# Two more token blocks of a gated layer in Strassen's seven-product form, with attention and weight decoding moved in the schedule

## Chip, cores and metric

One core of one Trainium2 chip runs the whole program in one launch. The metric is the device time of that launch in microseconds (us); lower is better. The time before is the median of three runs.

## What is computed

Pooled attention, then two gated layers, all in float32; the five weight matrices arrive as 64-bit floats. Cut to what matters:

```python
k_p = k.reshape(B, H, Sp, 8, D).mean(axis=3)         # B=8 batches, H=8 heads, S=576, D=64
v_p = v.reshape(B, H, Sp, 8, D).mean(axis=3)         # Sp = 72
attn = softmax(q @ k_p.T / sqrt(D))
x = (attn @ v_p) -> [B*S, H*D]                       # 4608 tokens x 512
x = ((x @ w_a) * (x @ w_b)) @ w_out                  # first layer, d_ff = 1536
h = x @ w_in                                         # second layer, d_ff = 2048
out = (h * clip(h + 3, 0, 6) / 6) @ w_out2
```

## The kernel before

**Tiling.** The 4608 tokens are NB = 9 blocks of 512 (TB). A matrix product in full precision is three matmuls of 128x128 by 512 (mm3, L724: high by high, low by high, high by low); block 0 alone uses single float32 matmuls. The two products x @ w_a and x @ w_b of the first layer are called the gates here.

**Plain blocks.** The first PLAIN = 5 blocks (L72) run step(j, f) (L932) for each of the NF1 = 12 slices f of 128 hidden columns: gate a into PSUM (pa), copied by ScalarE (asb, L959); gate b (pb), multiplied by VectorE (L982); the product split into a high and a low part (L84, L85); and y_part (L743), which adds the slice's share of the output in four PSUM banks that stay open over all 12 slices. The weights of gate b and of w_out come from DRAM in every block from block 2 on (w1_load, L719), those of gate a stay in SBUF.

**Superblocks.** The other blocks go in pairs of 1024 tokens, NSUP = (NB - PLAIN) // 2 of them. pair1(s, p) (L1498) runs six times in a superblock (NP1 = 6), each time on two slices f and for both gates m, over the seven products of Strassen's scheme (ORDER). x_prod (L1416) is one product of one gate: 2 x 3 matmuls. x_evict (L1433) takes results out of PSUM: ScalarE copies, VectorE adds and multiplies, GpSimd multiplies and subtracts. y_chunk (L1459) makes a 128-row share of the output for 512 tokens (2 x 3 matmuls), eight in a pair, which VectorE adds to an SBUF sum (ya, L1471) from the second pair on. The seven combinations of the weights (ab) are made once, in superblock 0, from the weights read back with t_load (L1300), by t_step (L1309), on ScalarE, VectorE and GpSimd, and stored to DRAM (tdram); later superblocks load them (L1320) LEAD = 3 products ahead. The combinations of the input are made by x_make (L1361) in seven pieces, from blocks that x_load (L1351) reads back from DRAM (xdram).

**The hand-made order.** Every engine and the DMA queue of SyncE (SP) work in the order in which this program issues. The clock of that order is the slot: a plain step has 3 slots, so a block has SLOTS = 36, and a pair of a superblock has 12, so a superblock has 72. With PLAIN = 5, superblock 0 starts at slot 180, superblock 1 at 252, and the second layer follows at 324. Attention is cut into 40 chunks of up to 128 tokens; `base` (L546 to L550) gives each chunk a first slot. The loop after it places the parts of a chunk: loads seven slots ahead, q_tr and scores (PE, VectorE), expo (ScalarE), sums, normal (GpSimd), at_main, at_left (PE, ScalarE, VectorE), and pv (PE, ScalarE), which for blocks from XD = 3 on stores the result to xdram. The first chunk of a batch also brings the pooling of k (k_prep, four VectorE reductions, nine to six slots ahead) and of v (v_prep, vl_prep). The 4 + 5 + 6 + 3 + 4 + 5 + 5 + 5 + 3 chunks of the blocks 0 to 8 start as follows: block 2 in slots 26 to 46, blocks 3 to 6 in slots 50 to 151, blocks 7 and 8 in slots 184 to 220. Batches 3, 4, 5 and 6 start within slots 50 to 151, batch 7 at 199. x_load and t_load of superblock 0 are at slots 166 and 169, its x_make pieces from 171 on.

**Weights of the second layer.** They are decoded from 64 bits and combined in 2 x NF2 = 32 steps: w2_stage (load), w2_decode and w2_end (ScalarE, VectorE, GpSimd), and for every two steps w2_sums (VectorE) and w2_make (ScalarE, VectorE, GpSimd, then stores to DRAM). W2_STEPS = 20 of them run in the plain blocks, one every two steps f from the fourth step of block 1 on; the other 12 in the last superblock, one every four slots (w2_slot, L1477).

run_slot(s, hold) (L629) issues what is planned for a slot; with hold it puts the pooling (k_prep, v_prep, vl_prep) off to run_held (L638).

Of the kernel before, what the change touches and what calls it, by code (L numbers as in the profile page):

```python
# [25 lines left out]
def pooled_attention_then_two_moe_kernel(  # L26
# [24 lines left out]
    NF2 = F2 // P  # L51
# [3 lines left out]
    NB = NT // TB  # L55
# [13 lines left out]
    ident = const.tile([P, P], F32, name="ident")  # L69
    masks = const.tile([P, 4], F32, name="masks")  # L70
    ydram = [dpool.tile([P, NCC, TB], F32, name=f"ydram{j}") for j in range(NB)]
    PLAIN = 5  # L72
    XD = 3
    NSUP = (NB - PLAIN) // 2
    xdram = {j: dpool.tile([P, NCC, TB], F32, name=f"xdram{j}") for j in range(XD, NB)}
# [430 lines left out]
    chunks, pieces, chunk_piece, block_chunks = [], [], {}, [[] for _ in range(NB)]  # L506
    for b in range(B):
        t = 0
        while t < S:
            j, r = divmod(b * S + t, TB)  # L510
            seg = S - t if b > 1 else min(S - t, TB - r)
            while seg:
                j = (b * S + t) // TB
# [16 lines left out]

    SLOTS = 3 * NF1
    SPAN2 = (26, 46)
    SPANS = ((50, 151), (184, 220))
    X_AT = 166
    T_AT = 169
    X0_AT = (171, 173, 174, 176, 177, 179, 180, 182)
    plan = {}

    def at(slot, fn, *args):
# [2 lines left out]
    def spread(cs, first, last):  # L542
        n = len(cs)
        return [first + i * (last - first) // max(1, n - 1) for i in range(n)]

    base = [None] * len(block_chunks[0])  # L546
    base += [4 * i + 6 for i in range(len(block_chunks[1]))]
    base += spread(block_chunks[2], *SPAN2)
    base += spread([c for j in range(3, PLAIN + 2) for c in block_chunks[j]], *SPANS[0])
    base += spread([c for j in range(PLAIN + 2, NB) for c in block_chunks[j]], *SPANS[1])  # L550
    att_used = {}
    WIDE = block_chunks[3][0]

# [10 lines left out]
    for c, (b, t0, n) in enumerate(chunks):  # L564
# [30 lines left out]
        x = place(max(s0, done) + 1, (scores, c, 0), (scores, c, 1))  # L595
# [4 lines left out]
        x = place(x + 5 + 2 * wide, (at_main, c), (at_left, c))  # L600
# [26 lines left out]
    held = []  # L627

    def run_slot(s, hold=False):  # L629
        now[0] = s  # L630
        calls = sorted(plan.pop(s, ()), key=lambda x: rank(x[0]))
        for fn, args in calls:
            if hold and fn in (k_prep, v_prep, vl_prep):
                held.append((fn, args))
            else:
                fn(*args)

    def run_held():  # L638
# [54 lines left out]

    AHEAD = 2
    W2_FROM = 3
    W2_STEPS = 20
    xd_t = {}

    def x_fetch(j):
# [774 lines left out]

    YWORK = (1, 1, 2, 1, 1, 1, 1)

    def w2_slot(x):  # L1477

        i, ph = divmod(x, 4)
        i += W2_STEPS  # L1480
        if x < 0 or i > 2 * NF2 + 1:
            return
        if ph == 0 and i < 2 * NF2:
            w2_stage(i)
        if W2_STEPS < i <= 2 * NF2:
            if ph == 1:
                w2_decode(i - 1)
            elif ph == 2:
                w2_end(i - 1)
        if i >= W2_STEPS + 2 and i % 2 == 0 and ph == 3:  # L1490
            w2_sums(i // 2 - 1, 0)
        if i >= W2_STEPS + 2 and i % 2 and ph in (0, 2):
            w2_make(i // 2 - 1, ph // 2)

    prev1 = []
    w2_late = []

    def pair1(s, p):  # L1498
# [3 lines left out]
        last = s == NSUP - 1  # L1502
# [4 lines left out]
        def hook(hold=False):  # L1507
            nonlocal section
            for u in range(section * 12 // 14, (section + 1) * 12 // 14):
                if u % 3 == 0:  # L1510
                    flush()
                if last and (p, u) == P2_AT:
                    attn_stack.close()
                    p2.append(ctx.enter_context(tc.tile_pool(name="p2", bufs=1)))
                if last and hold:
                    w2_late.append(4 * 3 * p + u - 6)
                elif last:
                    while w2_late:
                        w2_slot(w2_late.pop(0))
                    w2_slot(4 * 3 * p + u - 6)  # L1520
                run_slot(slot0 + u, hold)
            if not hold:
                while w2_late:
                    w2_slot(w2_late.pop(0))
                run_held()
            section += 1

# [94 lines left out]
```

## Time and profile before

| | us |
|---|---|
| median of 3 runs | 1738.91 |
| lowest and highest run | 1736.78, 1739.81 |
| span of the profiled execution, first to last instruction | 1736.1 |
| TensorE (PE) busy in it | 1701.8 |

Only the span of the profiled execution is on the page; its own time from outside is not given. The runs' median is 2.8 us above the span. Times within a profile count from the span's start. Stretches in it, read from the starts of the blocks' matmuls and evictions: block 1 from 181 to 307, block 2 to 427, block 3 to 541, block 4 to 643, superblock 0 to 832, superblock 1 to 1022, then the second layer. A view by windows gives the busy time of each engine in a stretch; a group of instructions gives their number and mean duration; PE's matmul durations overlap each other, so the rate of matmuls is read from how many lie in a stretch in which PE is never idle.

### The profile page before, as it was taken

What the parts mean: (1) busy time and instruction counts of PE and PEld (TensorE: products, weight loads), DVE (VectorE), ACT (ScalarE), POOL (GpSimd) and SP (SyncE); (2) the same over time, 40 slices, a digit from 0 to 9 for tenths busy, and PEclk for the clock granted to TensorE, in tenths of its full rate; (3) what the DMA queues carried; (4) which work ended last, traced back from release to release, by engine and by line L of the source; (5) the groups of instructions that cost most, each with busy time, mean ns of one, the idle gap of its engine ahead of it and who ended that gap; (6) DMA issues with size and microseconds to landing.
All of it is one profiled execution on the core that took longest, in us unless ns stands there. A gap on an engine that the chain in (4) does not pass through costs nothing.

```text
span 1736.1 us, 24577 instructions
## 1 busy us (share of the span) xinstructions
PE 1701.8 (98%) x7924; PEld 1371.8 (79%) x7924; DVE 1247.7 (72%) x1978; ACT 787.5 (45%) x1622; POOL 918.6 (53%) x779
## 2 busy tenths in 40 slices
PE   7989999999999999999999999999999999999998
PEld 5445788787887887888888877888888888888898
DVE  6777877667758467754666776687678768767776
ACT  6655444333334344443344434455445545544453
POOL 4565223113213147666545627686577668666753
PEclk9999999999999999999999999999999999999999
DMA  9774558796878667755688948465945976594896
GB/s 255 196 227 128 175 190 263 190 313 183 273 264 293 210 243 249 247 183 213 216 294 281 343 154 317 172 227 152 319 155 180 239 276 217 155 315 157 300 293 256
DMA packets 294480, 404.31 MB, mean 233 GB/s; under 512 B 157392, under 2 KB 197840, under 8 KB 294352
## 3 DMA queue, kind: packets, MB, share of 16 engines
q1 hardware_dynamic: 293920, 402.22, 71.2%
q8 instruction: 64, 1.05, 0.2%
q14 instruction: 64, 0.52, 0.1%
q10 hardware_dynamic: 432, 0.52, 0.1%
HBM read 307.23 MB, written 95.42 MB: 232 GB/s over the span
## 4 chain that ended last, share of the span: by engine, by line
PE 79%; DVE 7%; DMA 5%; issue 3%; SPq 2%; ACT 2%; POOL 2%; DVEq 0%; POOLq 0%; ACTq 0%
PE y L728 4%; PE y L726 4%; PE y L727 4%; PE oZ L728 4%; PE phZ L726 4%; PE oZ L726 4%; PE phZ L727 4%; PE phZ L728 4%; PE oZ L727 4%; PE phX L726 3%; PE phX L728 3%; PE phX L727 3%; PE oX L727 2%; PE oX L726 2%; PE oX L728 2%
## 5 line engine op out<-in xcount | busy, mean ns | idle before, releaser
L85 POOL TENSOR_TENSOR g<-r,g 128x512 fp32r<-128x512 f32 (+1 forms) x192 | 254.0, 1345 | 10.0 <-ACT g L84 10.0
L1161 POOL TENSOR_TENSOR r<-r,r 128x512 f32<-128x512 f32 (+1 forms) x39 | 47.2, 1211 | 181.1 <-DVE rT L1159 152.2
L98 POOL TENSOR_TENSOR w2f<-w2f,w2st 128x512 int32<-128x512 int32 x32 | 42.7, 1334 | 153.7 <-ACT w2st L91 101.9
L1192 DVE TENSOR_TENSOR oacc<-oZ,oacc 128x512 f32<-128x512 f32 (+1 forms) x130 | 82.5, 635 | 52.6 <-PE oZ L728 52.3
L726 PE MATMUL oZ<-g,wo 128*128 128x512 f32 (+1 forms) x320 | 118.4, 370 | 1.3 <-DVE oacc L1192 1.3
L728 PE MATMUL oZ<-g,wo 128*128 128x512 f32 (+1 forms) x320 | 118.5, 370 | 0.9 <-POOL g L85 0.5
L727 PE MATMUL oZ<-g,wo 128*128 128x512 f32 (+1 forms) x320 | 118.0, 369 | 0.0
L84 ACT CAST g<-r 128x512 fp32r<-128x512 f32 (+1 forms) x195 | 104.5, 576 | 16.4 <-DVE r L1163 15.9
L85 POOL TENSOR_TENSOR g<-rT,g 128x512 fp32r<-128x512 f32 (+1 forms) x77 | 98.1, 1275 | 20.5 <-ACT g L84 18.1
L1137 ACT ACTIVATE r<-phX 128x512 f32<-128x512 f32 (+1 forms) x78 | 43.2, 554 | 128.7 <-DVE phX L1131 126.5
L726 PE MATMUL phZ<-Sh,wi 128*128 128x512 f32 x256 | 99.9, 390 | 1.5 <-ACT r L1137 1.5
L1471 DVE TENSOR_TENSOR ya<-y,ya 128x512 f32<-128x512 f32 x80 | 54.9, 687 | 64.3 <-PE y L728 64.3
L728 PE MATMUL phZ<-Sl,wi 128*128 128x512 f32 x256 | 99.8, 390 | 0.0
L727 PE MATMUL phZ<-Sh,wi 128*128 128x512 f32 x256 | 99.7, 389 | 0.0
L959 ACT COPY asb<-pa 128x512 f32<-128x512 f32 x60 | 35.2, 586 | 114.6 <-PE pa L728 93.5
L726 PE MATMUL pa<-xh,wa 128*128 128x512 f32 x192 | 76.9, 400 | 0.0
L728 PE MATMUL y<-g,wo 128*128 128x512 f32 x192 | 75.0, 391 | 0.9 <-POOL g L85 0.8
L726 PE MATMUL phX<-Sh,wi 128*128 128x512 f32 x192 | 74.9, 390 | 0.5 <-ACT e L1127 0.5
L728 PE MATMUL pa<-xl,wa 128*128 128x512 f32 x192 | 75.1, 391 | 0.0
L727 PE MATMUL pa<-xh,wa 128*128 128x512 f32 x192 | 75.0, 391 | 0.0
L726 PE MATMUL y<-g,wo 128*128 128x512 f32 x192 | 74.9, 390 | 0.0
L728 PE MATMUL phX<-Sl,wi 128*128 128x512 f32 x192 | 74.9, 390 | 0.0
(947 smaller groups left out, 5491.5 us busy)
## 6 DMA issues: line engine op xcount, KB each, us to landing
wo<-wod SPq DMA_DIRECT2D x140, 512.0 KB
wi<-wsd SPq DMA_DIRECT2D x120, 512.0 KB
tdram<-ab SPq DMA_DIRECT2D x42, 512.0 KB
ab<-tdram SPq DMA_DIRECT2D x42, 512.0 KB
wod<-tt SPq DMA_DIRECT2D x56, 256.0 KB
wsd<-tt SPq DMA_DIRECT2D x24, 512.0 KB
wo<-w1dram SPq DMA_DIRECT2D x24, 512.0 KB
wi<-wsd SPq DMA_DIRECT2D x40, 256.0 KB
```

Source lines behind the costliest of these rows:

```text
L84: (hi_eng or nc.scalar.copy)(hi, src)
L85: (lo_eng or nc.gpsimd).tensor_tensor(lo, src, hi.bitcast(F32), ALU.subtract)
L98: nc.gpsimd.tensor_tensor(di, di, lo.bitcast(I32), ALU.add)
L726: nc.tensor.matmul(o, wh, xh, start=first, stop=False, skip_group_check=more)
L727: nc.tensor.matmul(o, wl, xh, start=False, stop=False, skip_group_check=more)
L728: nc.tensor.matmul(o, wh, xl, start=False, stop=last, skip_group_check=more)
L959: nc.scalar.copy(asb, pa)
L1137: nc.scalar.activation(r[:, :n], o, AF.Relu, bias=3.0)
L1161: nc.gpsimd.tensor_tensor(r["12"], r["12"], r["11"], ALU.subtract)
L1192: nc.vector.tensor_tensor(acc, o, acc, ALU.add)
L1471: nc.vector.tensor_tensor(acc, o, acc, ALU.add)
```

## The change

PLAIN becomes 3: blocks 3 and 4 are a superblock as well, so there are three, starting at slots 108, 180 and 252. Attention of the blocks of each superblock gets a span of its own: blocks 3 and 4 in slots 50 to 82, blocks 5 and 6 in 100 to 150, blocks 7 and 8 in 172 to 222. x_load and t_load of superblock 0 are both at slot 97, its x_make pieces at 100 to 110. Of the 32 decoding steps 8 run in the plain blocks, none in superblock 0, 12 in superblock 1 and 12 in superblock 2. In every superblock the decoding of a held hook now waits for the next one that is not held, and run_slot runs a held pooling when its own write comes up first. The combined weights are made in superblock 0 as before and loaded in two superblocks now.

```diff
-    PLAIN = 5
+    PLAIN = 3
...
-    SPANS = ((50, 151), (184, 220))
-    X_AT = 166
-    T_AT = 169
-    X0_AT = (171, 173, 174, 176, 177, 179, 180, 182)
+    SPANS = ((50, 82), (100, 150), (172, 222))
+    X_AT = 97
+    T_AT = 97
+    X0_AT = (100, 101, 102, 104, 105, 107, 108, 110)
...
-    base += spread([c for j in range(3, PLAIN + 2) for c in block_chunks[j]], *SPANS[0])
-    base += spread([c for j in range(PLAIN + 2, NB) for c in block_chunks[j]], *SPANS[1])
+    for i, span in enumerate(SPANS):
+        base += spread(block_chunks[PLAIN + 2 * i] + block_chunks[PLAIN + 2 * i + 1], *span)
...
             if hold and fn in (k_prep, v_prep, vl_prep):
                 held.append((fn, args))
             else:
+                for x in [x for x in held if {k_prep: k_write, v_prep: v_write, vl_prep: vl_split}[x[0]] == fn and x[1] == args]:
+                    held.remove(x)
+                    x[0](*x[1])
                 fn(*args)
...
-    W2_STEPS = 20
+    W2_STEPS = 8
+    W2_PART = 20
...
-    def w2_slot(x):
+    def w2_slot(s, x):
         i, ph = divmod(x, 4)
-        i += W2_STEPS
-        if x < 0 or i > 2 * NF2 + 1:
+        a, e = (W2_PART, 2 * NF2) if s == NSUP - 1 else (W2_STEPS, W2_PART)
+        i += a
+        if x < 0 or i > e + 1 or s < NSUP - 2:
             return
...
-                if last and hold:
+                if hold:
                     w2_late.append(4 * 3 * p + u - 6)
-                elif last:
+                else:
                     while w2_late:
-                        w2_slot(w2_late.pop(0))
-                    w2_slot(4 * 3 * p + u - 6)
+                        w2_slot(s, w2_late.pop(0))
+                    w2_slot(s, 4 * 3 * p + u - 6)
```

## Rows read from the trace of the kernel before

**Rows 1.** The page, part 1: busy us, share of span, instructions.

```profile
PE 1701.8 (98%) x7924; PEld 1371.8 (79%) x7924; DVE 1247.7 (72%) x1978; ACT 787.5 (45%) x1622; POOL 918.6 (53%) x779
```

**Rows 2.** Windows, one per stage: length, each engine's busy us, clock, DMA.

```profile
core 0: us, PE busy (x) PEld busy (x) DVE busy (x) ACT busy (x) POOL busy (x), PEclk, DMA share, GB/s
181.00:307.00 126.00, 124.34 (x610) 101.83 (x609) 98.32 (x181) 59.32 (x130) 35.49 (x40) 1.00 0.71 224
307.00:427.00 120.00, 115.73 (x563) 95.59 (x562) 83.75 (x147) 45.89 (x95) 28.86 (x27) 1.00 0.75 229
427.00:541.00 114.00, 112.83 (x543) 93.42 (x542) 79.55 (x145) 44.47 (x96) 29.75 (x30) 1.00 0.80 253
541.00:643.00 102.00, 102.00 (x480) 85.22 (x479) 62.57 (x95) 40.45 (x77) 27.00 (x23) 1.00 0.72 253
643.00:783.00 140.00, 138.13 (x666) 113.11 (x665) 97.42 (x176) 65.79 (x132) 100.61 (x87) 1.00 0.70 231
...
832.00:972.00 140.00, 139.90 (x616) 115.39 (x616) 91.04 (x131) 53.52 (x96) 70.70 (x54) 1.00 0.79 277
```

**Rows 3.** Matmul groups of the whole span: count, busy, mean ns.

```profile
L726 PE MATMUL pa<-xh,wa 128*128 128x512 f32 x192 | 76.9, 400 | 0.0
...
L726 PE MATMUL pZa<-xSh,ab 128*128 128x512 f32 x96 | 37.8, 394 | 0.3 <-ACT k L1450 0.3
```

**Rows 4.** Windows of short dense stretches, columns as in rows 2.

```profile
180.00:220.00 40.00, 38.34 (x188) 29.73 (x187) 35.91 (x57) 18.25 (x42) 8.43 (x10) 1.00 0.68 210
...
820.00:840.00 20.00, 20.00 (x90) 16.54 (x90) 19.68 (x18) 9.77 (x14) 16.31 (x8) 1.00 0.57 211
...
1000.00:1020.00 20.00, 20.00 (x90) 16.56 (x89) 19.54 (x28) 8.95 (x13) 7.25 (x6) 1.00 0.47 173
1060.00:1080.00 20.00, 20.00 (x89) 16.53 (x89) 13.43 (x19) 8.35 (x15) 12.57 (x11) 1.00 1.02 405
```

**Rows 5.** VectorE's groups in 643 to 832: count, busy us, mean ns.

```profile
L1471 DVE TENSOR_TENSOR ya<-y,ya 128x512 f32<-128x512 f32 x29 | 20.0, 689 | 30.2 <-PE y L728 30.2
...
L153 DVE TENSOR_REDUCE kp<-kraw 72x128 f32<-72x1024 f32 x4 | 7.8, 1979 | 0.0
...
L342 DVE TENSOR_TENSOR sme<-mx,sc 128x288 f32<-128x288 f32 x12 | 5.5, 454 | 0.7
...
L296 DVE STREAM_TRANSPOSE qT<-qraw 128x128 f32<-128x128 f32 x24 | 5.2, 273 | 0.0
L359 DVE TENSOR_REDUCE su<-sme 128x8 f32<-128x584 f32 x6 | 4.5, 749 | 0.0
...
L427 DVE TENSOR_TENSOR atl<-atm,ath 128x512 fp32r<-128x512 f32 x6 | 4.1, 683 | 5.3 <-ACT ath L426 5.3
...
L153 DVE TENSOR_REDUCE vs<-vraw 128x128 f32<-128x1024 f32 x2 | 3.9, 2006 | 0.0
...
L442 DVE TENSOR_TENSOR atx<-atl,atx 32x256 fp32r<-32x256 f32 x6 | 2.5, 423 | 0.2
```

**Rows 6.** The decoding's split on VectorE in 307 to 427, a plain block.

```profile
L85 DVE TENSOR_TENSOR tt<-w2s,tt 128x512 fp32r<-128x512 f32 x3 | 2.1, 686 | 1.3 <-ACT tt L84 1.3
```

**Rows 7.** The same group in 900 to 980, in superblock 1.

```profile
L85 DVE TENSOR_TENSOR tt<-w2s,tt 128x512 fp32r<-128x512 f32 x5 | 6.1, 1228 | 0.0
```

**Rows 8.** Timeline of SP's queue at superblock 0's loads: start us, us, issue.

```profile
594.37 4.58 SPq L148 DMA_DIRECT2D xdram<-xo  x4
...
601.01 4.62 SPq L1358 DMA_DIRECT2D xr<-xdram  x4
```

**Rows 9.** Timeline of VectorE, first use of those loads.

```profile
619.35 1.22 DVE L1381 TENSOR_TENSOR xT<-xr,xr 128x1024 f32<-128x1024 f32 x1
```

**Rows 10.** SP's waits in 832 to 972: total us, times, longest us.

```profile
SPq L143 <- DVE tt L85: 46.7, 7, 15.2
```

**Rows 11.** Timeline of SP's queue in superblock 1: two loads of combined weights.

```profile
878.30 0.32 SPq L1320 DMA_DIRECT2D ab<-tdram  x1
...
895.77 0.40 SPq L1320 DMA_DIRECT2D ab<-tdram  x1
```

More of the change, by code (lines that the diff above doesn't have):

```diff
@@ L1475, in pooled_attention_then_two_moe_kernel @@
     YWORK = (1, 1, 2, 1, 1, 1, 1)
-    def w2_slot(x):
+    def w2_slot(s, x):
         i, ph = divmod(x, 4)
-        i += W2_STEPS
-        if x < 0 or i > 2 * NF2 + 1:
+        a, e = (W2_PART, 2 * NF2) if s == NSUP - 1 else (W2_STEPS, W2_PART)
+        i += a
+        if x < 0 or i > e + 1 or s < NSUP - 2:
             return
-        if ph == 0 and i < 2 * NF2:
+        if ph == 0 and i < e:
             w2_stage(i)
-        if W2_STEPS < i <= 2 * NF2:
+        if a < i <= e:
             if ph == 1:
@@ L1489, in w2_slot @@
                 w2_end(i - 1)
-        if i >= W2_STEPS + 2 and i % 2 == 0 and ph == 3:
+        if i >= a + 2 and i % 2 == 0 and ph == 3:
             w2_sums(i // 2 - 1, 0)
-        if i >= W2_STEPS + 2 and i % 2 and ph in (0, 2):
+        if i >= a + 2 and i % 2 and ph in (0, 2):
             w2_make(i // 2 - 1, ph // 2)
@@ L1523, in hook @@
                 while w2_late:
-                    w2_slot(w2_late.pop(0))
+                    w2_slot(s, w2_late.pop(0))
                 run_held()
```

## Prediction

> **What bounds the kernel now.** I read three views. First the page's totals: PE is busy for 1701.8 of 1736.1 us, VectorE (DVE) 72% of the time, the others less [rows 1]. So only matmuls taken away, or idle time of PE, can move the end: 34 us are idle in all. Second the windows by stage: the clock is at full speed (1.00, the level of 2.4 GHz) throughout, and PE's idle time from block 1 to slot 42 or so of superblock 1 is the length less the busy time: 1.7, 4.3, 1.2, 0.0, 1.9 and 0.1 us [rows 2]. The stages that the change touches are PE-bound already. Third, what stands closest behind PE: DVE, at 70% of the plain block 2, 70% of the attention stretch of superblock 0 and 65% of the stretch of superblock 1 in which weights are decoded [rows 2]. The reader should keep that: attention and decoding lie in different superblocks today, and DVE is not full in either.
>
> **What is removed: matmuls.** A plain block issues 12 x 3 x 4 x 3 = 432 of them (12 slices; gate a, gate b, output; 4 chunks; 3 matmuls). A superblock issues six times 7 x 2 x 6 = 84 for the gates and 8 x 6 = 48 for the output: 792 for two blocks instead of 864. The counts of the trace agree with the code: 192 first matmuls of gate a are 4 blocks x 48, 96 of pZa are 2 superblocks x 6 x 8 [rows 3]. So 72 fewer. Their price is the rate of a stretch without idle time: 90 in 20.00 us [rows 4], 0.222 us each (the 390 to 400 ns of a group overlap). **-16.0 us**, all on the path, since PE has no slack. The second layer and the attention keep their matmuls.
>
> **What is added beside PE.** A superblock costs DVE 15 operations of 0.69 us in a pair (six adds, one product, eight ya) [rows 5], 62 us in six pairs, and two plain blocks cost 24 x 2 x 0.69 = 33. GpSimd gains seven operations in a pair. SP loses 48 loads of gate-b and output weights and 4 of x, and gains 42 of combined weights, 12 of output weights and 4 of x, all of 512 KB: 58 for 52. As totals these are hidden. What counts is where they fall, so I take the stages in order.
>
> **Plain blocks.** Block 1 keeps its attention up to slot 62 and its 1.7 us. Block 2 keeps batch 4 (its k_prep at 67 to 70 instead of 72 to 75) and one chunk every 5 slots instead of 6; I keep its 4.3 us. Block 3 with its 1.2 us is gone: **-1.2 us**.
>
> **The earlier start of superblock 0.** Before, the four xr loads left at 601 to 605.6, and their first use on DVE was at 619.4, without idle time in front [rows 8, 9]: 14 us after the last left. Now x_load stands 3 slots, some 8.5 us (102 us for 36 slots in block 4 [rows 2]), ahead of the first piece instead of 5, and the last store of block 4 (pv at slot 93) 4 slots ahead of x_load as before. Two t_load and two weight loads share the queue. At 4.6 us for the issue of four [rows 8] the third, which the first piece also needs, leaves about 4 us before its use, and 512 KB at the 405 GB/s of the trace's busiest stretch [rows 4] take 1.3 us. Late or not is open: 0 to 4 us, a gain is excluded since the same loads stand in both. ScalarE and DVE wait in order there, and the plain step's asb and pb are queued behind them. I take **+1 us**, near the lower end.
>
> **Superblock 0 with two batches.** From the groups one chunk costs DVE 2 x 0.45 (sme) and as much for its minimum, 4 x 0.27 (qT), 0.75 (su), 0.68 (atl), 0.42 (atx) [rows 5]: 4.8 us for a full one; two in eight are half chunks, so 4.5 in the mean. A batch costs 4 x 1.98 + 3 x 2.0 = 14 us. These are upper values, since neighbours overlap a little. The 140 us from 643 hold 8 chunks and one batch, 50 us of the 97.4 us busy [rows 2]. The new ones (slots 108 to 161) hold 9.5 chunks and the batches 5 and 6: 43 + 28 = 71. So DVE is busy for 97.4 - 50 + 71 = 118 of 140 us, 85%. PE loses 1.9 us there at 70%. The densest 40 us that the trace has beside attention lost 1.7 us at 90% [rows 4], 4.1%, 5.8 us on this length. Between the two bounds I take 4.6: **+2.7 us**.
>
> **Superblock 1 with attention and decoding together.** This is the step on which most hangs, and no stretch of the trace shows the mix. Today's superblock 1 has the same decoding at the same slots (6 to 54): DVE 91.0 of 140 us, PE idle 0.1 [rows 2]. The change adds batch 7 and seven chunks (slots 180 to 233): 14 + 31.5. DVE: 136.5 of 140 us, 98%. Its order is fixed, and PE needs it often: the next pair's first product waits for the last eviction, which it follows closely, and the y chunks have two free PSUM banks while X is in use. Behind a 2 us reduction [rows 5] such evictions come late. From below: two stretches of 20 us ran with DVE at 98% and PE never idle [rows 4], which would give 0. From above: if it can be kept only as busy as in the 40 us at 90%, the work takes 136.5 / 0.90 = 152 us, +12; at 88% it takes 155, +15. I take 93%, nearer to the long stretch than to the short ones, since backlog carries 20 us but not 140: 147 us, **+7 us**. Behind it superblock 2 is today's superblock 1 without attention, and hides its decoding as that does.
>
> One operation changes its price with the place. The split of the decoding on DVE takes 686 ns in block 2, where GpSimd is busy 24% of the time, and 1228 ns in superblock 1, where it is busy 50% [rows 2, 6, 7]. I take superblock 1's price for the 12 steps there, as the 91.0 us already hold it. The Trainium skill, GPSIMD Engine Reference, section 1 "Specifications", says that GpSimd shares its SBUF interfaces with VectorE and contends with instructions that have two SBUF inputs. The row agrees, and the rule speaks against this change, because the attention's normal() runs on GpSimd too. By it I would let the 24 two-input operations of these 12 steps grow by another fifth of the 0.54 us, 2.6 us as an estimate from that page, and the time would be 1735 instead of 1732; the sum does without it.
>
> **Sum.** -16.0 - 1.2 + 1 + 2.7 + 7 = -6.5 us. The span's 1736.1 becomes 1729.6. What lies between the span and the runs' median (2.8 us) is untouched, so the median of 1738.9 becomes **1732 us**.
>
> **Rivals.**
> - *Only the arithmetic.* DVE stays ahead in both superblocks, as in the two 98% stretches, and no stall is added: 1738.9 - 16.0 - 1.2 = 1722 us. For it: PE's idle time hardly follows DVE's share (70% cost 4.3 us in block 2 and 1.2 us in block 3, 65% cost 0.1) [rows 2]. Against it: those stretches are short.
> - *DVE becomes the bound of superblock 1.* At 88% it adds 15 instead of 7: 1740 us, no change that could be told. It decides if the stretch has more idle places in DVE's order than the 40 us at 90% had.
> - *SP's queue makes it slower.* SP issues in order, and in superblock 1 it stands in front of decoding stores until DVE has made them: seven waits, 46.7 us, the longest 15.2 [rows 10]. One such wait put 17.5 us between two loads of combined weights [rows 11], although one is needed every 4.5 us (187 us for 42 products). Nothing was lost because loads had been issued ahead. Now k, v, q and xdram transfers enter the same queue, and the pool of 28 buffers must also hold them beside 14 input parts. From the point where a load leaves less than its own time before its product, every wait stalls PE: at 3.5 us for each of seven, 24.5 us instead of 7 give 1750 us, slower. Against it: the traffic, 277 GB/s [rows 2] and about 1 MB a chunk in 19 us more, stays below the 405 GB/s that cost nothing [rows 4].
> - *The saving does not come*, because the rate of matmuls falls in superblocks: against it, the 90 in 20 us stand in superblocks [rows 4]. About 1739 us.
>
> **How the numbers follow.** Forecast (1728 to 1737) 0.43, only the arithmetic 0.22, DVE as the bound 0.18, SP's queue 0.14, no saving 0.03. A measurement of this kernel can tell about 0.2%, 3.5 us, from no change. Faster by more (below 1735.4): 0.22 and four fifths of 0.43, together 0.57. Slower by more (above 1742.4): 0.14 and a fifth of 0.18, together 0.17. Within: 0.26. The range goes from the arithmetic alone, 1721, to the DVE bound at 86% (159 us, +19), 1745; it leaves out the queue's case and little else.
>
> **What would show it.** Right: three superblocks whose PE-busy time without attention is 176 us each (792 x 0.222); DVE above 90% from slot 180 to 233 of the new count and PE idle there for 4 to 10 us, released by DVE, with less in superblock 0 and next to nothing in superblock 2; the first xSh copy of superblock 0 waiting on a DMA for at most some us. Wrong: PE idle in superblock 1 released by loads of combined weights (the queue), or hardly any idle time (arithmetic alone), or long idle time in blocks 1 and 2, where I changed nothing although attention is denser there.

## The result and the profile after

The changed kernel takes 1763.1 us (four runs, 1761.0 to 1765.4), the kernel before, measured beside it, 1738.7 us: 1.0144 times as long, 95% interval 1.0131 to 1.0156. It is slower by 24 us where 1732 us, 7 us faster, was forecast, and it lies above the forecast's range, which ended at 1745.

The profiled execution, the shortest of the four, spans 1759.2 us, 23.1 more than before. The first line below is part 1 of the page (the counterpart of [rows 1]), the second the view of the cores.

```profile
PE 1697.3 (96%) x7852; PEld 1363.8 (78%) x7852; DVE 1282.7 (73%) x2016; ACT 800.0 (45%) x1643; POOL 982.9 (56%) x824
```

```profile
core 0: 1759.2 us, clock 0.992
```

The 72 matmuls are gone (7924 to 7852), and yet PE's busy time fell by 4.5 us only. PE's idle time rose from 34.3 to 61.9 us, and the mean granted clock fell from 1.000 to 0.992. The windows by stage say where; the columns are those of [rows 2]: blocks 1 and 2, then the three superblocks.

```profile
181.00:305.00 124.00, 120.73 (x593) 98.45 (x592) 104.56 (x185) 58.53 (x130) 36.64 (x38) 1.00 0.66 203
305.00:418.00 113.00, 111.40 (x539) 92.98 (x538) 73.39 (x130) 45.43 (x89) 30.30 (x30) 1.00 0.79 263
418.00:637.00 219.00, 203.65 (x957) 166.42 (x956) 150.38 (x242) 97.27 (x195) 144.10 (x117) 0.98 0.65 213
637.00:863.00 226.00, 208.97 (x951) 170.59 (x950) 164.38 (x265) 90.38 (x177) 113.44 (x94) 0.96 0.77 250
863.00:1044.00 181.00, 180.81 (x796) 148.83 (x795) 123.16 (x178) 72.25 (x126) 87.70 (x68) 1.00 0.78 273
```

Blocks 1 and 2 (4.9 us idle) and the third superblock (0.2 us) lose no more than before. The first two superblocks lose 15.4 and 17.0 us of idle time, and the clock is below 1.00 in both. DVE, the engine I feared, is busy for 69% and 73% of them and nowhere near 98%.

The waits of PE in these two stretches (engine, line and tile, what it waited for: us in total, times, longest) are nearly all attention's.

```profile
PE ktp L174 <- DVE kp L153: 11.4, 4, 5.7
PE atm L424 <- DVE sme L342: 1.6, 1, 1.6
PE pXa L731 <- POOL ab L1310: 1.6, 1, 1.6
...
```

```profile
PE atm L424 <- DVE sme L342: 6.7, 1, 6.7
PE sc L331 <- DVE atl L427: 3.4, 1, 3.4
PE sc L331 <- DVE qT L296: 2.4, 1, 2.4
PE sc L331 <- ACT w2f L90: 1.2, 1, 1.2
PE pZb L730 <- DVE k L1455: 1.1, 1, 1.1
PE y L732 <- POOL g L85: 1.0, 1, 1.0
...
```

ktp is the transpose of a pooled key (k_write), sc the scores, atm the transpose of the softmax. They have a fixed place in PE's order, between matmuls of the superblock, and those behind them wait with them. Each needs something from DVE: the pooled row kp, or one of attention's two PSUM banks ("att"), which comes free when DVE has read it. The first fence is superblock 0, the second superblock 1; what is left out is 0.5 and 1.0 us. No load of SP is among these waits.

The timeline shows what stands ahead on DVE. First the start of superblock 0, the third row of batch 5's keys (start, duration, engine, instruction, idle time before it): the line of PE's step, then DVE's lines in their order.

```profile
436.27 0.35 PE L174 MATMUL ktp<-ident,kp 72*128 72x72 f32 x1 [5.75 <-DVE kp L153]
...
428.59 1.21 DVE L1380 TENSOR_TENSOR xSl<-xr,xSh 128x1024 fp32r<-128x1024 f32 x1
429.72 0.75 DVE L359 TENSOR_REDUCE su<-sme 128x8 f32<-128x584 f32 x1
430.50 0.20 DVE L362 RECIPROCAL rc<-su 128x8 f32<-128x8 f32 x1
430.74 0.69 DVE L1448 TENSOR_TENSOR k1a<-pWa,k1a 128x512 f32<-128x512 f32 x1
431.35 0.68 DVE L1449 TENSOR_TENSOR k1b<-pWb,k1b 128x512 f32<-128x512 f32 x1
431.94 0.61 DVE L296 STREAM_TRANSPOSE qT<-qraw 128x64 f32<-128x64 f32 x4
432.48 3.64 DVE L153 TENSOR_REDUCE kp<-kraw 72x128 f32<-72x1024 f32 x2
```

The pooled row stands behind an input piece, a softmax sum, two evictions and a transpose, and PE waits 5.75 us for it. DVE has no gap in all this time. Now superblock 1, the scores (sc), the step that waits (atm), and DVE's order between them:

```profile
708.39 2.26 PE L331 MATMUL sc<-bd,qT 128*128 128x144 f32 x8 [2.42 <-DVE qT L296]
719.33 0.45 PE L424 MATMUL atm<-ident,am 128*128 128x128 f32 x1 [6.75 <-DVE sme L342]
...
708.76 1.99 DVE L214 SCALAR_TENSOR_TENSOR vml<-vs,vmh 64x128 fp32r<-64x128 f32 x2
710.78 1.96 DVE L153 TENSOR_REDUCE vls<-vlraw 96x128 f32<-96x1024 f32 x1
713.16 0.28 DVE L248 TENSOR_TENSOR vlhl<-vls,vlhl 32x128 fp32r<-32x128 f32 x1 [0.42 <-ACT vlhl L247]
713.47 0.69 DVE L1448 TENSOR_TENSOR k6a<-pXa,k6a 128x512 f32<-128x512 f32 x1
714.08 0.68 DVE L1449 TENSOR_TENSOR k6b<-pXb,k6b 128x512 f32<-128x512 f32 x1
714.68 0.68 DVE L1473 COPY ya<-y 128x512 f32<-128x512 f32 x1
715.27 1.38 DVE L102 SCALAR_TENSOR_TENSOR w2f<-w2st,w2f 128x512 uint32<-128x512 uint32 x1
716.58 1.75 DVE L85 TENSOR_TENSOR tt<-w2s,tt 128x512 fp32r<-128x512 f32 x1
718.25 0.45 DVE L336 TENSOR_REDUCE mx<-sc 128x4 f32<-128x288 f32 x1
718.73 0.45 DVE L342 TENSOR_TENSOR sme<-mx,sc 128x288 f32<-128x288 f32 x1
```

The scores are in PSUM at 710.65, but DVE reads them from 718.25 on: batch 7's values (4.2 us), three evictions (2.1) and two pieces of decoding (3.1) come first, 9.4 us in all, and PE stands 6.75 us for the bank. The wait is the part of this that PE could not fill: 7.6 us of DVE's order are left when the scores are done, the two operations that free the bank (mx, sme) bring DVE to 719.3, and PE had only six matmuls of a product, to 712.6, in between. The window of these 11 us: DVE is full here (10.45 us), in a superblock in which it is busy for 73%, and the mean granted clock is 0.67.

```profile
708.00:719.00 11.00, 4.19 (x14) 3.47 (x14) 10.45 (x16) 2.92 (x8) 7.07 (x7) 0.67 0.64 191
```

The lower clock follows these idle times. Five windows of 20 us, columns as above:

```profile
420.00:440.00 20.00, 13.41 (x55) 9.97 (x56) 15.49 (x19) 8.91 (x20) 12.90 (x8) 0.88 0.79 251
440.00:460.00 20.00, 19.84 (x94) 15.66 (x93) 14.20 (x26) 11.26 (x23) 16.32 (x14) 0.95 0.99 314
...
700.00:720.00 20.00, 10.83 (x45) 8.79 (x43) 19.28 (x28) 6.28 (x15) 10.14 (x9) 0.79 0.74 232
720.00:740.00 20.00, 20.00 (x83) 16.31 (x83) 11.95 (x24) 9.97 (x19) 9.73 (x9) 0.87 0.65 220
740.00:760.00 20.00, 16.60 (x78) 13.76 (x77) 11.16 (x21) 5.74 (x12) 4.60 (x6) 0.91 0.68 205
```

In the 20 us from 720 PE is never idle but gets through 83 matmuls where [rows 4] show 90.

### The profile page after: what moved, and what is told of

The parts are those of the page before. It is cut to its first block, busy times and chain, and to the rows that moved or that the text cites. A ratio compares the mean times of both kernels' runs of the same rounds, so it can differ in the third digit from the quotient of the medians.

```text
span 1759.2 us, 24602 instructions
## 1 busy us (share of the span) xinstructions
PE 1697.3 (96%) x7852; PEld 1363.8 (78%) x7852; DVE 1282.7 (73%) x2016; ACT 800.0 (45%) x1643; POOL 982.9 (56%) x824
## 4 chain that ended last, share of the span: by engine, by line
PE 74%; DVE 10%; DMA 8%; SPq 2%; issue 2%; POOL 2%; ACT 2%; DVEq 0%; ACTq 0%; POOLq 0%
PE oZ L732 4%; PE oZ L730 4%; PE y L732 4%; PE oZ L731 4%; PE y L730 4%; PE y L731 4%; PE phZ L730 4%; PE phZ L731 4%; PE phZ L732 4%; PE phX L731 3%; PE phX L730 3%; PE phX L732 3%; PE oX L731 2%; PE oX L730 2%; PE oX L732 2%
## 5 line engine op out<-in xcount | busy, mean ns | idle before, releaser
L1475 DVE TENSOR_TENSOR ya<-y,ya 128x512 f32<-128x512 f32 x120 | 82.4, 687 | 100.3 <-PE y L732 100.1
L732 PE MATMUL y<-g,wo 128*128 128x512 f32 x288 | 112.7, 391 | 1.2 <-POOL g L85 1.0
L730 PE MATMUL y<-g,wo 128*128 128x512 f32 x288 | 113.0, 392 | 0.0
L731 PE MATMUL y<-g,wo 128*128 128x512 f32 x288 | 112.7, 391 | 0.0
L1450 POOL TENSOR_TENSOR k5a<-k5a,k5b 128x512 f32<-128x512 f32 x18 | 24.5, 1362 | 91.4 <-DVE k5b L1449 78.2
L730 PE MATMUL phX<-Sh,wi 128*128 128x512 f32 x192 | 74.9, 390 | 0.4 <-ACT e L1131 0.4
L731 PE MATMUL phX<-Sh,wi 128*128 128x512 f32 x192 | 74.7, 389 | 0.0
L1196 DVE TENSOR_TENSOR oacc<-oX,oacc 128x512 f32<-128x512 f32 (+1 forms) x70 | 44.4, 634 | 35.5 <-PE oX L732 35.5
```

The costliest lines, as they stand in the source:

```text
L730: nc.tensor.matmul(o, wh, xh, start=first, stop=False, skip_group_check=more)
L731: nc.tensor.matmul(o, wl, xh, start=False, stop=False, skip_group_check=more)
L732: nc.tensor.matmul(o, wh, xl, start=False, stop=last, skip_group_check=more)
L1196: nc.vector.tensor_tensor(acc, o, acc, ALU.add)
L1450: nc.gpsimd.tensor_tensor(ta, ta, tb, ALU.mult)
L1475: nc.vector.tensor_tensor(acc, o, acc, ALU.add)
```

## The experiments

All are edits of the changed kernel, and times stand against its 1763.1 us; the kernel before, measured beside each, gave 1737.8 to 1739.1 us. Stage times are those of one profiled execution, whose total can lie some microseconds from the median. Theory A: PE stands at attention's steps because what frees them is queued locally behind other work on DVE. Theory B: the sum of DVE's load in a superblock decides. (In e1 and e2 Theory A is narrower: single long operations in front. Theory C there is loads that come late.) Slots: the superblocks start at 108, 180 and 252. Where an expectation below says that attention starts 14 slots into its superblock, read 14 slots later than in the change, 6 slots in.

**Work left out, one suspect at a time.** e1: sum8 copies one row instead of summing eight, for batches 5 to 7. e2: DVE's part of the 12 decoding steps of superblock 1, except the splits, which stay on it.

```diff
     def sum8(dst, t, eng=None, b=0):
+        if b >= 5:
+            nc.vector.tensor_copy(dst, t.rearrange("p g (j d) -> p g j d", j=POOL)[:, :, 0])
+            return
```

> The changed kernel with the sums of eight rows for batches 5, 6 and 7 left out: each of the seven VectorE reductions of 2.0 us of a batch becomes a copy of one row of the eight (about 0.2 us), everything else stays in its place. 12.6 us of VectorE time leave each batch. Theory A (single long operations at the head of VectorE's queue: PE waits for one of them or for what stands behind it, and each such wait also lowers the granted clock for some us): of the 33 us of PE idle time in superblocks 0 and 1, the 11.4 us on ktp and most of the 12 us behind v_prep go, and the clock stays at 1.00: 1763 - 20 to 28 = 1735 to 1743. Theory B (VectorE's total load in a superblock): superblock 0 goes from 150 to 125 us busy and recovers, superblock 1 only from 164 to 152: 1763 - 15 = about 1748. Theory C (loads that come late through SP's queue): nothing changes, 1758 to 1765, since the loads stay.

```diff
     def w2_end(i):
         st, t = w2st.pop(i)
-        decode_end(t, st)
+        if not W2_STEPS <= i < W2_PART:
+            decode_end(t, st)
```
(and the same condition in w2_decode, w2_sums and w2_make)

> The changed kernel with VectorE's decoding work of the 12 steps in superblock 1 left out (clamp, shift, last merge and the sums; 12 x 2.3 us + 6 x 2.3 us = 41 us); ScalarE's, GpSimd's, the splits' and the DMA work stays. That is as much VectorE time as the seven reductions of three batches, but in pieces of 0.4 to 1.4 us. Theory A (long operations in front): superblock 1 keeps part of its waits around v_prep, 5 to 10 us of its 17 us of idle time come back, superblock 0 nothing: 1750 to 1757. Theory B (total load): superblock 1 falls from 164 to 123 us busy and loses nothing any more, its 17 us and its lower clock come back: 1735 to 1740, superblock 0 unchanged with 15 us idle. Theory C (late loads): 1758 to 1765.

e1: 1744.3 us, -18.8, just above Theory A's range: superblock 0 takes 207 us instead of 219 (idle 6.8), superblock 1 takes 221 and keeps a wait of 6.6 us at atm. e2: 1750.5 us, -12.7, in Theory A's range and not in B's: superblock 0 keeps its 15.4 us, superblock 1 takes 212 us (idle 8.8) and keeps a 6.3 us wait at atm. Neither alone is the cause: where one piece goes, others are still queued ahead of the bank's release. In e1 the reduction in front of atm shrank from 2.0 to 0.2 us and the wait hardly did: PE's scores ran in 1.2 us instead of 2.3, so the value pieces (2.0 us) that had run beside them now stood for the greater part behind them.

**Another engine.** e4 pools batches 5 to 7 on GpSimd (below for k; v likewise); e7 gives the softmax of blocks 5 to 8 to ScalarE, as in blocks 0 and 1.

```diff
-        sum8(kp, t, None if b else nc.vector)
+        sum8(kp, t, nc.gpsimd if b >= 5 else None if b else nc.vector)
```

> The changed kernel with the pooling of batches 5, 6 and 7 on GpSimd (three additions each) instead of one VectorE reduction of 2.0 us each. VectorE loses 14 us a batch, GpSimd gains an estimated 2.6 us x 7 = 18 us a batch (additions of 512, 256 and 128 elements at its 1.3, 0.8 and some 0.5 us): superblock 0 goes from 144 to 180 us busy of 219 there, superblock 1 from 113 to 131. Theory A: the waits for kp on VectorE go, but in superblock 0 GpSimd now delays the low parts of the combined weights; 5 to 20 us come back in all: 1743 to 1758. Theory B: as much, superblock 0 above all. Theory C: unchanged, 1758 to 1765. If it comes below 1739 it is a version to go on from.

```diff
     act_chunks = set([c for c in block_chunks[0] if c != 2] + block_chunks[1])
+    act_chunks |= {c for j in range(5, NB) for c in block_chunks[j]}
```

> The changed kernel in its own order, with the softmax of the chunks of blocks 5 to 8 in the form that blocks 0 and 1 have: ScalarE takes the exponential with the row's minimum as bias and the sum in the same instruction (eight per chunk), instead of a difference and a sum on VectorE (2 x 0.45 + 0.75 us) and one exponential on ScalarE. VectorE loses 1.65 us a chunk, 16 us in superblock 0 and 12 in superblock 1, in short pieces; ScalarE, busy 40 to 45%, gains some 2 us a chunk; PE's bank for the scores is freed by ScalarE. Theory A (long operations and what stands together): part of the waits of sc and atm behind sme go, those on kp stay: 1763 - 4 to 10 = 1753 to 1759. Theory B (total load): 28 us less on VectorE, more than two thirds of what the missing reductions gave, which was 19 us: 1763 - 13 = 1750 or below.

e4: 1775.4 us, +12.2. e7: 1770.7 us, +7.6. Both take load off DVE, both are slower, and both lie above every range in their expectations. The windows of e7's first two superblocks:

```profile
420.00:650.00 230.00, 209.78 (x950) 170.29 (x951) 143.12 (x222) 113.53 (x335) 140.24 (x114) 0.94 0.62 204
650.00:875.00 225.00, 208.29 (x949) 169.57 (x948) 156.35 (x251) 102.79 (x281) 112.42 (x94) 0.96 0.76 250
```

DVE has 7 and 8 us less to do in them, and PE is idle for 20.2 and 16.7 us. The waits behind the pieces that moved went with them, to GpSimd (e4, superblock 0) and to ScalarE (e7, superblock 1):

```profile
PE ktp L174 <- POOL kp L158: 16.8, 4, 11.0
```

```profile
PE atm L424 <- ACT sme L307: 7.7, 1, 7.7
```

The keys cost 16.8 us instead of 11.4, and atm 7.7 instead of 6.7. That speaks against Theory B: what counts is when the releasing queue gets to the piece, whichever engine's it is.

**Spread out.** e3 starts attention's spans 14 slots later and leaves their ends; e5 is e3 with the pooling of batches 5 to 7 every third slot and PE's transpose of a key three slots behind it instead of two; e6 is e5 with the decoding of superblock 1 spread over 70 slots; e8 is e6 with e7's softmax.

```diff
-    SPANS = ((50, 82), (100, 150), (172, 222))
+    SPANS = ((50, 82), (114, 151), (186, 222))
```

> The changed kernel with attention of blocks 5 and 6 in slots 114 to 151 instead of 100 to 150, and of blocks 7 and 8 in 186 to 222 instead of 172 to 222: all chunks stand closer (4 slots instead of 5.5, 5 instead of 7), but none lies beside the x_make pieces and the first pair of a superblock. Nothing else differs. Theory A (what stands together at a place): the 8 us of idle time at 428 to 437 and the lower clock behind them go, 5 to 12 us come back: 1751 to 1758. Theory B (VectorE's load over a stretch): the same load in three quarters of the time, so more idle time: 1768 to 1785.

```diff
+            if b >= 5:
+                k_at, v_at = [s0 - 14, s0 - 11, s0 - 8, s0 - 5], [s0, s0 + 3, s0 + 6]
```

> The kernel with the moved attention spans (114 to 151, 186 to 222), and in it the pooling of batches 5, 6 and 7 pulled apart: k_prep every third slot (14, 11, 8 and 5 slots ahead of the chunk) instead of every slot, its write to PE three slots behind it instead of two, v_prep every third slot. No work is added or taken away. Theory A (what stands together at a place in VectorE's order): the waits on kp (5.7 us of PE idle time there) go, those behind v_prep shrink: against 1756 for the moved spans alone 4 to 10 us less, 1746 to 1752. Theory B (VectorE's load over a superblock): unchanged within 3 us, 1753 to 1759.

```diff
-                    w2_slot(s, 4 * 3 * p + u - 6)
+                    for x in w2_at(s, 12 * p + u):
+                        w2_slot(s, x)
```
(w2_at gives superblock 1 its 56 phases over 70 slots)

> As the run before, and the 12 decoding steps of superblock 1 spread over 70 of its 72 slots instead of 52 (one step every five slots instead of four), from its first slot on. Same work. Theory A: the wait of 6 us in the second pair of superblock 1 (attention's minimum and difference queued behind decoding and v) shrinks, 3 to 6 us less than the run before: 1742 to 1748. Theory B: the same load in superblock 1, no change, 1746 to 1752.

> All three together: moved spans, pooling pulled apart, decoding spread over superblock 1, softmax of blocks 5 to 8 on ScalarE. Theory A: most places at which VectorE's queue is full are thinned, 12 to 16 us less than with the spans alone: 1738 to 1744, beside 1738 of the kernel before. Theory B: the loads fall only by the 28 us of the softmax: 1743 to 1750. Below 1735 it would be a version that beats both.

e3: 1756.0 us, -7.1, although attention is denser: superblock 0 takes 212 us, superblock 1 takes 231. e5: 1754.5 us, -1.4 against e3, which taken alone is Theory B's range: the waits for keys are gone, but in superblock 0 scores waited 9.9 us for banks, and in superblock 1 PE waited 5.0 us for one load of combined weights, which it had not done in the changed kernel. e6: 1762.9 us, 8.4 worse than e5: superblock 1 takes 4 us more, the other two 3 us more each, and the load still comes 5.3 us late. That the slower decoding stands beside more of the attention is a reading, not shown. e8: 1770.8 us, as bad as e7. e6 and e8 miss both theories' ranges. Spreading does not help by itself.

**Pooling elsewhere.** e9 keeps all work and pools batch 5 in block 2 (slots 84 to 95) and batch 7 late in superblock 0 (153 to 164).

```diff
+            if b in (5, 7):
+                e0 = {5: 84, 7: 153}[b]
+                k_at, v_at = [e0 + 2 * i for i in range(NP)], [e0 + 7 + 2 * i for i in range(3)]
```

> Change kept whole; only the pooling of batch 5 is issued earlier (in block 2, whose VectorE was 58 to 65% busy) and that of batch 7 in the first superblock's second half, so that no row of pooled keys is asked for by TensorE just after a superblock begins, and the second superblock has no batch-7 pooling beside the decoding. VectorE's work is the same in sum. Theory A (TensorE stands at attention's transposes and scores because what frees their banks is queued behind other work on VectorE): first superblock's idle time 15.4 -> about 7, second's 17 -> about 10, and with the clock 1745 to 1753. Theory B (sum of VectorE's load decides): 1760 to 1766, since the sum over the two superblocks falls by the pooling moved out only (some 14 us of 315).

e9: 1755.3 us, -7.8, less than Theory A's numbers. Superblock 1 takes 216 us (226), its wait at atm falls from 6.7 to 1.9 us. Superblock 0 stays at 220 us: batch 5's waits are gone, batch 6's are as before (4.9 of the 8.5 us for keys), and batch 7's keys (3.6) now make PE wait there too; blocks 1 and 2 take 243 us in place of 237.

**Decoding elsewhere.** e10 leaves 4 of the 12 steps in superblock 1 and gives the rest to superblock 2, at 1.5 phases a slot; e11 is e9 and e10; e12 adds e3's spans.

```diff
-    W2_PART = 20
+    W2_PART = 12
...
+    def w2_at(s, t):
+        return [t] if s < NSUP - 1 or t < 0 else range(t * 3 // 2, (t + 1) * 3 // 2)
```

> Change kept whole; of the decoding steps that stood in the second superblock 4 stay and the others go to the third, which has no attention and VectorE idle for most of its time. Theory A: the second superblock loses its decoding as in the run without decoding work (idle 17 -> about 9) and the third takes it without an idle TensorE: 1748 to 1754, close to 1750.5 of the run that left the work out. Theory B, the work costs wherever it stands beside GpSimd's and matmul's evictions: 1758 to 1764.

> The two before together. Theory A: the idle times are at different places, so the gains add: 1733 to 1744, and the first two superblocks' idle time together under 18 us (32.4 in the changed kernel). If the 6.5-us wait at the transpose of the softmax stays because some other piece on VectorE takes the decoding's place, 1745 to 1752.

> The two before together, and attention starting 14 slots after the superblock does (the spans of the earlier run that gained 7 us). Theory A: another 3 to 7 us off where the first slots of a superblock still carry the pieces of its inputs: 1728 to 1740. If denser attention costs more than the start gains once pooling is moved, 1740 to 1750.

e10: 1782.0 us, +18.9; e11: 1776.6; e12: 1763.7. All miss. Superblock 1 behaves as expected: 226 us in the change, 216 with either move, 208 with both; the two gains add. But superblock 2's gate products take 208 us instead of 179, without any attention. PE's wait and DVE's in e10's superblock 2, and its window:

```profile
PE pZb L730 <- DVE k L1455: 11.4, 3, 4.4
...
DVE w2f L102 <- POOL w2f L98: 16.9, 15, 1.6
```

```profile
859.00:1066.00 207.00, 189.06 (x782) 153.44 (x781) 156.39 (x222) 87.00 (x156) 105.15 (x81) 0.94 0.84 295
```

With two phases in every other slot DVE itself waits for GpSimd's part of a decoding step, 15 times and 16.9 us (4 times and 5.9 us in the change), and in the two longest of the three waits at pZb (4.4 and 3.8 us) such a step stands ahead of the product k that frees the bank. It is the same mechanism without attention, at another bank, and again with the clock (0.94).

**How much is left.** e13 is e9 with e3's spans; e14 is e13 with 8 steps of decoding in superblock 1 and 16 in superblock 2, at 9 phases for 8 slots; e15 is e13 with the work left out that e1 and e2 leave out.

> Change kept whole, with batch 5's and 7's pooling earlier and attention starting 14 slots after its superblock; decoding stays where the change has it (12 steps in the second superblock, 12 in the third). If the gains of the two moves (7.8 and 7.2 us) are at different places: 1747 to 1750. If they remove the same waits: 1753 to 1757. The third superblock goes back from 205 us to 181 to 183 in either case.

```diff
-    W2_PART = 20
+    W2_PART = 16
...
+        return [t] if s < NSUP - 1 or t < 0 else range(t * 9 // 8, (t + 1) * 9 // 8)
```

> As the run before, with 8 decoding steps in the second superblock and 16 in the third, at 9 phases for every 8 slots there. If it was density (1.5 phases per slot in the runs that lost 19 us) that cost the third superblock its 25 us, it now loses less than 6 and the second gains 3 to 5: 1745 to 1751. If every decoding step beyond 12 costs the third superblock some 3 us wherever it stands: 1755 to 1762.

> As the first run of this set, and of batches 5 to 7 the row sums are left out (one row copied in their place), and of the second superblock's twelve decoding steps VectorE's work; the output is not the reference's. It bounds what attention's other steps cost beside superblock matmuls. If pooling and decoding with the order they stand in are the whole loss: 1720 to 1728, both superblocks under 192 us, clock at 0.999 or above. If the chain of transposes, scores, softmax and evictions costs by itself, because each step stands in TensorE's order before VectorE has freed its bank: 1733 to 1742, with 6 us or more idle in each of the first two superblocks.

e13: 1745.6 us, -17.5, a little more than the two gains (-7.1, -7.8) together. e14: 1764.3 us, a miss at 18.7 us over e13: superblock 1 gains 3 us, but the last decoding pieces fall into the last pair, where the second layer's inputs are made on DVE. Superblock 2's gate products take 192 us instead of 179, 7 us more pass before the second layer's first matmul, and in these two stretches PE waits 4.2 us for DVE's ya, 4.8 for its k and 6.1 for the split of the product (g). Density is thus not the only thing that makes decoding dear there; I have not separated the rest. e15: 1720.4 us. Its cores, page and the windows of its first two superblocks:

```profile
core 0: 1717.8 us, clock 1.000
```

```profile
PE 1683.9 (98%) x7852; PEld 1357.4 (79%) x7852; DVE 1224.3 (71%) x1956; ACT 799.4 (47%) x1643; POOL 976.2 (57%) x824
```

```profile
415.00:619.00 204.00, 200.83 (x971) 166.15 (x971) 140.54 (x250) 97.80 (x196) 143.17 (x119) 1.00 0.72 236
619.00:822.00 203.00, 201.44 (x953) 166.95 (x952) 115.85 (x203) 85.85 (x160) 109.11 (x94) 1.00 0.80 266
```

The clock does not fall in any stage, and attention's other steps cost 3.2 and 1.6 us of idle time. (I had expected under 192 us for a superblock and forgot that attention's own matmuls are in it.) In its superblock 0 DVE is busy 69% of the time, exactly as in the changed kernel, and PE loses 3.2 instead of 15.4 us: the share alone does not tell the loss.

**PE asks later.** e16 is e13 with the pooling of batches 5 and 7 three slots apart and ktp four slots behind its sum instead of two; e17 is e16 with superblock 1's decoding four slots earlier; e18 takes e13's places for batch 5 and e16's for batch 7.

```diff
-                done = max(done, place(k_at[hp] + (3 if b == 1 else 2), (k_write, b, hp)))
+                done = max(done, place(k_at[hp] + (3 if b == 1 else 4 if b == 7 else 2), (k_write, b, hp)))
```
(e18's line; in e16 and e17 it is `b in (5, 7)`)

> As the run with both moves and the decoding left in place (1745.6), and for batches 5 and 7 the row sums stand 3 slots apart and TensorE's transpose of the pooled keys 4 slots behind its sum in place of 2. All work is kept. If the place in TensorE's order is the cause: the two waits for pooled keys (5.3 us) and the lower clock behind them (some 4 us) go, 1735 to 1741. If the reductions themselves slow whatever else VectorE serves: the waits move to scores or softmax transposes, 1743 to 1748.

> As the run before, and the second superblock's decoding starts 4 slots earlier, away from its attention. If the 3.4-us wait at the softmax's transpose there comes from a decoding step that stands ahead of the softmax on VectorE, it changes its size by its place: 1733 to 1745; if nothing but the number of decoding steps counts: within 2 us of the run before.

> All work kept. Batch 5 is pooled in block 2 at slots 84 to 95 (where the run with both moves lost nothing), batch 7 from slot 149 on, 3 slots apart with TensorE's transposes 4 slots behind; attention starts 14 slots into its superblock; decoding as in the changed kernel. If the gains add by place: 1745.5 less the 7 us that block 2 lost in the run with both batches spread, 1736 to 1740, no difference that can be told from the kernel before. If the first superblock's gain hung on batch 5's later rows: 1743 to 1747.

e16: 1745.5 us, no gain over e13. The waits for keys are gone and superblock 0 takes 208 us instead of 216, but blocks 1 and 2 give 7 us back: the last pieces of batch 5's values, with input pieces and a decoding split, now stand ahead of an eviction there (PE's pb waited 5.2 us for DVE's gl). e17: 1749.8 us, 4.3 worse than e16, outside both expectations. The profiled executions differ by 3.1 us, 1.1 of it in superblock 1, where the waits at pZb rose from 1.9 to 6.5 us while others fell, and 2.1 in blocks 1 and 2, where nothing was changed. That the place of the decoding makes the 4.3 us is not shown. e18: 1737.9 us (11 runs), ratio to the kernel before 0.9998, interval 0.9989 to 1.0007. Its windows:

```profile
181.00:415.00 234.00, 229.52 (x1114) 189.15 (x1113) 188.57 (x307) 107.40 (x235) 68.20 (x66) 1.00 0.75 239
415.00:624.00 209.00, 202.99 (x969) 167.97 (x969) 159.07 (x250) 96.89 (x196) 147.10 (x118) 0.98 0.71 230
624.00:840.00 216.00, 206.08 (x951) 168.34 (x950) 154.74 (x263) 85.69 (x159) 111.39 (x94) 0.98 0.75 251
```

All work kept, only places in the schedule moved: the whole loss of the change is given back, 25 us, while DVE's busy time in superblock 0 rose from 150 to 159 us and stayed at 314 to 315 us in the first two superblocks together. With the same load and 25 us less, the sum of the load cannot be what decides. The kernel is level with the one before and does not beat it; 17.5 us still lie between it and e15.

## Why the prediction was wrong, point by point

Between the kernel before, e15 and the change the sum can be written with measured terms. With all matmuls of the change at full clock, e15's PE is busy for 1683.9 us, 17.9 less than before. The changed kernel issues the same 7852 matmuls in 1697.3 us, 13.4 us more, which is the lower clock. Its idle time is 27.6 us above that of before. -17.9 + 13.4 + 27.6 = +23.1 us, the difference of the spans.

- *Matmuls removed, -16.0*: right. Measured 17.9; the price of 0.222 us was a little low.
- *Blocks 1 to 3, -1.2*: right in the sum. Blocks 1 and 2 idle 4.9 us instead of the 6.0 of [rows 2], but as 3.3 and 1.6 us where 1.7 and 4.3 were kept; that they make up for each other is luck.
- *Earlier start of superblock 0, +1*: not needed. The loads were issued from 382.5 us on, and ScalarE's first xSh copy began at 394.8 without idle time before it.
- *Superblock 0 with two batches, +2.7*: **the first step that failed.** 15.4 us idle and not 4.6. The DVE work was right, 118 us in slots 108 to 161, but I read PE's loss off DVE's mean share: that stretch took 166 us and DVE was busy for 71% of it, not 85%. e15 has the same share over the superblock as the changed kernel and loses 3.2 us.
- *Attention and decoding together, +7*: **the second.** 17.0 us idle. "DVE kept busy 93%" pictured a queue that is never empty and PE slowed in step. In fact DVE is 73% busy in slots 180 to 233 (127 of 174 us): PE stands at one fixed step, and while it stands it makes nothing that DVE could work on later. The wait is set by what is ahead in DVE's order at that point, 9.4 us in the row of 708 to 718. The 98% itself was too high, for two reasons. Superblock 1 of the kernel before began with its first product at 840.45 us, not at 832, so the stretch of [rows 2] starts with 8 us of superblock 0, in which DVE was full [rows 4], and ends at slot 53, not 42. Taken from 840, as below, DVE has 82.3 us of work, 128 with attention added. And that work was set against a length without attention's own matmuls: e15, with 1.6 us of idle time, takes 152 us for these slots. 128 of 152 us is 84%, and even so PE lost 17 us.

```profile
840.00:971.00 131.00, 130.90 (x577) 107.95 (x576) 82.31 (x122) 48.90 (x89) 64.51 (x50) 1.00 0.79 278
```

- *The clock*: **the missing term.** All rows of before showed 1.00, and I put no price on a fall. It cost 13.4 us, about half a microsecond for each added microsecond of idle time; the other runs, set against e15 in the same way, show 0.4 to 0.8 (e18 1.3), so this is no fixed price. More than half of the gap between e18 and e15 is of this kind: e18's PE is busy 10.7 us longer than e15's for the same matmuls, of 19.2 us between the spans.
- *Superblock 2 hides its decoding*: right, 0.2 us idle in 181. That it has no room for more, as e10 and e14 showed, the prediction did not ask.
- *GpSimd and DVE*: the split of the decoding (tt from w2s) took 1202 ns in the mean in superblock 1, against the 1228 of [rows 7], and all two-input operations of the twelve steps 38.7 us against 39.3. The 2.6 us of that estimate are not seen. GpSimd did more work there (113 us instead of 95) in a longer time, and was busy for the same half of it, so no run shows what a higher share would cost. The Trainium skill, GPSIMD Engine Reference, section 1 "Specifications", says that GpSimd shares its SBUF interfaces with VectorE, with contention for instructions that have two SBUF inputs; the trace agrees in so far as the split costs 0.69 us in block 2 [rows 6] and 1.20 us here.

Of the rivals, *only the arithmetic* (1722) is what e15 measures when most of the pooling and decoding is out of DVE's way and the rest stands at e13's places (1720). *SP's queue* (1750) came nearest in time, but for the wrong reason: no wait of PE in the first two superblocks is for a DMA. The queue is not free of it for ever: in e5 and e6 one load came 5 us late. *DVE as the bound* named the right engine and the wrong quantity. Of the signs I set up, "PE idle in superblock 1, released by DVE" came, with two and a half times the size forecast; "DVE above 90%" did not, and "less in superblock 0" hardly did (15.4 against 17.0 us).

Two of the chances are a hundredth off: 0.22 and four fifths of 0.43 are 0.56, 0.14 and a fifth of 0.18 are 0.18.

What stays open: why each decoding step beyond twelve costs superblock 2 so much (e14's 18.7 us for four steps), what made e17 slower than e16, and how e18's last waits could go; its longest is 4.3 us at a softmax transpose, behind ScalarE's eviction of attention's output.

## What to carry to other kernels

When work moves beside a busy TensorE, don't price it by the share of the engine that serves it: list, for each step of TensorE that needs a buffer or a row from that engine, what stands ahead of it in that engine's order, and add up what is left of it when TensorE gets there; 9 us there were a 7 us stall at 73% load. Ask for a result several slots after its producer is issued, and move the few long pieces (pooling) to stretches where nothing else is due; here the place was worth 25 us with the work unchanged. Then price each idle time twice, once for itself and once for the lower clock that these traces show behind it.

## What the runs showed of the hardware

The granted clock had been 1.00 in every row of the kernel before. In the changed kernel it was 0.67 in the mean of the 11 us in which PE mostly stood at atm, a window that mixes the levels of 2.4 and 1.2 GHz, and 0.87 in the 20 us from 720, in which PE was busy throughout. Matmuls of 512 columns took 0.63 us there and after the wait at 436 us, against the usual 0.39.

The prediction reckoned with contention between DVE and GpSimd for two-input operations only. An operation with one input is stretched too: below, GpSimd's product and DVE's first decoding piece overlap. Line L96 took 426 ns in the median of superblocks 1 and 2 and L1450 1289 ns.

```profile
704.68 1.66 POOL L1450 TENSOR_TENSOR k5a<-k5a,k5b 128x512 f32<-128x512 f32 x1 [10.23 <-DMA ab<-tdram]
705.12 1.51 DVE L96 TENSOR_SCALAR w2f<-w2f 128x512 f32<-128x512 f32 x1
```

Both are longer together, 1.3 and 3.5 times their medians. The trace of the changed kernel holds 32 pieces of L96 from 181 us on: the 22 beside which GpSimd ran nothing of more than 0.3 us took at most 0.43 us, the ten that overlapped with such an operation 0.44 to 1.52. That the overlap is the cause is read from these times; no run varied it alone.
